# Splitting a V load of 128 partitions into one of 120 and one of 8, in an attention forward and backward kernel

## The chip, the cores and the metric

The kernel runs on one core of a Trainium2 chip. A core has TensorE (PE, whose weight loads are listed apart as PEld), VectorE (DVE), ScalarE (ACT), GpSimd (POOL) and SyncE (SP), which here issues every transfer, and 16 DMA engines that move the data between HBM and the on-chip memory SBUF. The metric is the device time of one execution in microseconds (us). Before the change it is 1648.51 us, the median of three runs (1648.39, 1648.51 and 1654.82).

## The reference

Two independent attention blocks, A and B, of the same shape, forward and backward. Per block there are 8 batches of 96 queries, 32 heads of width 128, and caches k and v of 512 keys. All in bfloat16. Cut to what matters:

```python
def _A_ref(x, k_cache, v_cache, wq, wo):            # _B_ref is the same
    B, Sq, D = x.shape                              # 8, 96, 640
    H, Dh = 32, 128                                 # Sk = 512
    q = (x @ wq).reshape(B, Sq, H, Dh).transpose(0, 2, 1, 3)
    scores = jnp.einsum("bhqd,bhkd->bhqk", q, k_cache) * (Dh ** -0.5)
    p = softmax(scores, axis=-1)
    o = jnp.einsum("bhqk,bhkd->bhqd", p, v_cache)
    return o.transpose(0, 2, 1, 3).reshape(B, Sq, H * Dh) @ wo

out = jnp.concatenate([A, B], axis=-1)
grads = vjp(out)(grad_out)      # dx, dk, dv, dwq, dwo of both blocks
```

The output and all ten gradients are returned. The caches are by far the largest inputs, and their gradients the largest outputs.

## The kernel before

**Tiling.** The unit of work is a chunk: one head of one batch of one block. A chunk has 96 queries on one side and 512 keys on the other. There are 2 x 32 x 8 = 512 chunks. Time is counted in ticks, one chunk a tick. Two neighbouring heads of a batch form a pair (HP = 2) and share their transfers, so that there are 256 pairs.

**Stages of a chunk.** c_s2a makes the scores S (L314) from Q and the transposed K and their maximum; c_s2b the exponential; c_s3a and c_s3b the probabilities P (L346, on GpSimd); c_s4 dV from P and dO (L387), which ScalarE copies to dV_sb (L392); c_s45 the output O from V and the transposed P (L362) and, in the same PSUM bank, the transpose of the next P (L369); c_s6 dP from the transposed V (L411) and dS (L415); c_s7 dK (L453), which ScalarE copies to dK_sb (L458); c_s78 dQ from K (L430) and the transpose of dS (L437). Between the chunks stand the steps of a head: projections (L250), natural copies, dwo (L491), dwq (L511), and groups of four heads that are multiplied with wo and wq into the output and dx (L536).

**Transfers.** Each pair needs V and K twice. Once they come transposed, KT_p and VT_p, by a transposing DMA (p_ldT, L277). Once they come as they are, V_sb and K_sb (p_ldn, L288): 128 partitions, each with four neighbouring keys of the two heads, so that a partition receives two runs of 1024 bytes, 256 KB in all. The gradients dV_sb and dK_sb go out in the same form (p_st, L297). A pair so has six transfers; in addition there are wq and wo slices (L199, L210), dwq and dwo (L518, L497), and inputs and outputs of x, the gradient and the result (L135, L141, L148, L552).

**Order.** Every step is put on a list with a tick and a slot, and the list is sorted. All transfers go through one chain on SyncE: the helper `sp` makes each one follow the one before it in issue order. For a pair whose first chunk has tick ct, the dictionary OFF has KT at ct-3, V at ct+1, VT at ct+2, K at ct+4, the store of dV at ct+7 and that of dK at ct+10. V is first read by c_s45 at ct+5, VT by c_s6 at ct+6, K by c_s78 at ct+9. Within SyncE's queue the six of different pairs interleave as KT, V, store of dV, VT, K, store of dK.

**Buffers.** V_sb, K_sb and VT_p have four buffers each, KT_p five, dV_sb four, dK_sb three. A load waits for the last reader of the buffer that it fills, a store for the copy that fills its tile. Completion is counted on eight semaphores in turn, so that each transfer also waits for the eighth before it.

The lines that the change touches are in p_ldn:

```python
    t_ = kvp.tile([128, HP, KC, 128], BF16, name=key, bufs=4)
    src = (kc if which == 0 else vc)[b, h:h + HP]
    sp(nc.sync.dma_start(t_[:].rearrange("p h c d -> p h (c d)"), src.rearrange("h (p c) d -> p h (c d)", c=KC)))
```

Of the kernel before, what the change touches and what calls it, by code (L numbers as in the profile page):

```python
# [77 lines left out]
def build_block(tc, em, tick0, blk, x, kc, vc, wq, wo, g_all, out_all, dx, dk, dv, dwq, dwo, ident, ones, pools, HG=4, first=True, groups=None):  # L78
    nc = tc.nc
# [7 lines left out]
    KC = Sk // 128  # L87
# [38 lines left out]
    sp = pools["sp"]  # L126
# [156 lines left out]
    def p_ldn(h, b, which):  # L283
        def f():
            key = "K_sb" if which == 0 else "V_sb"
            t_ = kvp.tile([128, HP, KC, 128], BF16, name=key, bufs=4)
            src = (kc if which == 0 else vc)[b, h:h + HP]
            sp(nc.sync.dma_start(t_[:].rearrange("p h c d -> p h (c d)"), src.rearrange("h (p c) d -> p h (c d)", c=KC)))  # L288
            for j in range(HP):
                CS[(blk, h + j, b)][key] = t_[:, j]  # L290
        return f
# [266 lines left out]
    for g in range(NG):  # L558
        h0 = GH0[g]
        for hh in range(groups[g]):  # L560
            h = h0 + hh
# [185 lines left out]
```

## Time and profile before

| What | us |
|---|---|
| Median of the runs | 1648.51 |
| The profiled execution, whole | 1642.09 |
| Its span, first to last instruction | 1640.3 |
| V_sb load, issue to landing (least, median, most) | 3.0, 4.3, 6.0 |
| K_sb load, the same | 3.0, 4.3, 6.7 |
| Transposing loads, the same | 3.1, 5.0, 7.4 |
| Stores of dV and dK, the same | 2.1, 4.4, 6.9 |
| Issue of a V_sb load on SyncE (least, median, most) | 0.38, 0.53, 1.68 |
| Issue of a transposing load (least, most) | 1.10, 3.94 |

The profile is of one execution, which was 6 us shorter than the median of the timed runs. Busy shares are parts of the span. A waits row tells which instruction waited, for whom, how long in total, how many times and the longest. SyncE does nothing but issue transfers, and its time is not counted as busy; the timeline of its queue shows each issue with its start and length. The DMA line gives, in 40 slices, the mean busy share of the 16 DMA engines; the queue rows give packets, megabytes and share. Queue q1 carries the program's own transfers, q8 and q14 carry instructions.

### The profile page before, as it was taken

To read this page: it belongs to the slowest core of one execution; us is meant where nothing else is said; L and a number is where in the kernel's file an instruction comes from. 1 tells how busy PE (TensorE), PEld (TensorE's weight loads), DVE (VectorE), ACT (ScalarE), POOL (GpSimd) and SP (SyncE) were. 2 spreads that over 40 slices of the span, in tenths; PEclk is the share of its full clock that TensorE was granted. 3 is DMA by queue.
4 is the path that set the end of the run, shared out by engine and by line. 5 is a ranking of instruction groups with operands and counts; after the bars stand their busy time and mean duration, and the time that the engine had idled before them with its cause. 6 is when DMAs were issued, how large, how long until landed. Compare 5 with 4: busy or idle time off the path is not lost.

```text
span 1640.3 us, 55387 instructions
## 1 busy us (share of the span) xinstructions
PE 1602.0 (98%) x20713; PEld 1262.0 (77%) x20906; DVE 1340.0 (82%) x3406; ACT 1346.9 (82%) x3498; POOL 532.3 (32%) x1026
## 2 busy tenths in 40 slices
PE   8899999999999999999999999999999999999998
PEld 6777877878777787777777778777787777877776
DVE  5876888888888888878778778888888888888796
ACT  7889988879788788877868889788788888889783
POOL 1333333333333333333323333333333333333331
PEclk9999999999999999999999999999999999999999
DMA  9999999999999999999999999999999999999995
GB/s 263 261 293 273 292 291 282 275 275 279 276 292 289 290 280 282 280 276 258 284 289 311 289 288 273 290 290 283 275 287 278 272 290 287 281 292 285 284 267 167
DMA packets 375566, 458.12 MB, mean 279 GB/s; under 512 B 40704, under 2 KB 367104, under 8 KB 367104
## 3 DMA queue, kind: packets, MB, share of 16 engines
q1 hardware_dynamic: 375296, 454.57, 103.2%
q8 instruction: 163, 2.67, 0.7%
q14 instruction: 107, 0.88, 0.1%
HBM read 160.10 MB, written 159.12 MB: 195 GB/s over the span
## 4 chain that ended last, share of the span: by engine, by line
PE 89%; DMA 4%; ACT 4%; issue 2%; DVE 1%; SPq 0%; POOL 0%; ACTq 0%; DVEq 0%
PE o_ps L536 12%; PE q_ps L250 12%; PE dwq_ps L511 6%; PE dK_ps L453 6%; PE dV_ps L387 6%; PE S_ps L314 6%; PE dwo_ps L491 6%; PE dP_ps L411 6%; PE optp_ps L362 5%; PE optp_ps L369 5%; PE dq_dst_ps L430 5%; PE dq_dst_ps L437 5%; PE n_ps L265 3%; PE nat_ps L477 2%; DMA out_dram<-dK_sb 2%
## 5 line engine op out<-in xcount | busy, mean ns | idle before, releaser
L401 POOL TENSOR_TENSOR prod<-OT_h,dOT_h 128x96 bf16<-128x96 bf16 x512 | 187.1, 365 | 824.4 <-DVE rinv L336 438.2
L346 POOL TENSOR_SCALAR P_sb<-E_sb,rinv 96x512 bf16<-96x512 bf16 x508 | 349.8, 689 | 252.5 <-DVE rinv L336 252.1
L458 ACT ACTIVATE dK_sb<-dK_ps 128x512 bf16<-128x512 f32 x512 | 305.4, 597 | 149.6 <-PE dK_ps L453 130.9
L326 ACT ACTIVATE E_sb<-S_ps,negm 96x512 bf16<-96x512 f32 x512 | 350.9, 685 | 65.1 <-DVE negm L316 51.8
L316 DVE TENSOR_REDUCE negm<-S_ps 96x1 f32<-96x512 f32 x512 | 347.6, 679 | 67.2 <-PE S_ps L314 66.5
L415 DVE SCALAR_TENSOR_TENSOR dS_sb<-dP_ps,dl_ps,P_sb 96x512 bf16<-96x512 f32 x512 | 380.6, 743 | 1.6 <-PE optp_ps L369 1.4
L392 ACT ACTIVATE dV_sb<-dV_ps 128x512 bf16<-128x512 f32 x512 | 307.2, 600 | 3.9 <-PE dV_ps L387 2.6
L376 ACT ACTIVATE PT_sb<-optp_ps 128x384 bf16<-128x384 bf16 x512 | 255.2, 499 | 1.7 <-PE optp_ps L369 0.8
L439 DVE COPY dST_sb<-dq_dst_ps 128x384 bf16<-128x384 bf16 x512 | 177.5, 347 | 53.1 <-PE dq_dst_ps L437 51.5
L387 PE MATMUL dV_ps<-dOnat_h,P_sb 96*128 96x128 bf16 x2048 | 199.7, 219 | 2.1 <-DVE ob L546 1.0
L453 PE MATMUL dK_ps<-Qnat_h,dS_sb 96*128 96x128 bf16 x2048 | 198.9, 219 | 0.1
L411 PE MATMUL dP_ps<-VT_p,dOT_h 128*96 128x512 bf16 x512 | 195.8, 382 | 0.0
L314 PE MATMUL S_ps<-KT_p,QT_h 128*96 128x512 bf16 x512 | 194.0, 379 | 0.5 <-ACT E_sb L326 0.2
L453 PEld LDWEIGHTS <-dS_sb 96*128 96x128 bf16 x2048 | 147.5, 97 | 48.3 <-issue 0.6
L430 PE MATMUL dq_dst_ps<-dST_sb,K_sb 128*128 128x96 bf16 x2048 | 171.8, 205 | 3.0 <-ACT dK_sb L458 2.8
L369 PE MATMUL optp_ps<-ident,P_sb 96*128 96x96 bf16 x2048 | 172.4, 206 | 2.2 <-DVE P_sb L346 1.6
L362 PE MATMUL optp_ps<-PT_sb,V_sb 128*128 128x96 bf16 x2048 | 169.6, 204 | 3.0 <-ACT PT_sb L376 0.9
L437 PE MATMUL dq_dst_ps<-ident,dS_sb 96*128 96x96 bf16 x2048 | 171.8, 205 | 0.0
L536 PE MATMUL o_ps<-wo_r,OT_h 128*128 128x128 bf16 (+1 forms) x722 | 144.5, 294 | 2.4
L536 PE MATMUL o_ps<-wqT_h,dQT_h 128*128 128x512 bf16 (+1 forms) x720 | 144.2, 294 | 2.5
L362 PEld LDWEIGHTS <-V_sb 128*128 128x128 bf16 x2048 | 107.6, 96 | 50.7 <-issue 3.4
L491 PE MATMUL dwo_ps<-g_nat,Onat 128*128 128x128 bf16 (+1 forms) x735 | 129.4, 297 | 4.3 <-ACT dK_sb L458 2.6
(75 smaller groups left out, 3044.7 us busy)
## 6 DMA issues: line engine op xcount, KB each, us to landing
out_dram<-dV_sb SPq DMA_DIRECT2D x256, 256.0 KB, 4.4
out_dram<-dK_sb SPq DMA_DIRECT2D x256, 256.0 KB, 4.5
V_sb<-in_A_v_cache_dram SPq DMA_DIRECT2D x128, 256.0 KB, 4.3
K_sb<-in_A_k_cache_dram SPq DMA_DIRECT2D x128, 256.0 KB, 4.4
V_sb<-in_B_v_cache_dram SPq DMA_DIRECT2D x128, 256.0 KB, 4.3
K_sb<-in_B_k_cache_dram SPq DMA_DIRECT2D x128, 256.0 KB, 4.3
out_dram<-ob SPq DMA_DIRECT2D x88, 160.0 KB, 4.1
out_dram<-dwq_sb SPq DMA_DIRECT2D x32, 320.0 KB, 4.9
```

The source lines that it names most:

```text
L314: nc.tensor.matmul(S_ps[:], hs["QT_h"][:, tok], st["KT"], start=True, stop=True)
L316: nc.vector.tensor_reduce(negm[:], S_ps[:], axis=AX.X, op=ALU.max, negate=True)
L326: nc.scalar.activation(E_sb[:].rearrange("q (a f) -> q a f", f=F4), st["S_ps"][:].rearrange("q (f a) -> q a f", f=F4), ACT.Exp, bias=st["n ...
L346: eng.tensor_scalar(P_sb[:], st["E_sb"][:], st["rinv"][:], 0.0, op0=ALU.mult, op1=ALU.add)
L362: nc.tensor.matmul(OT_ps, st["V_sb"][:, c, :], st["PT_sb"][:, c * Sq:(c + 1) * Sq], start=(c == 0), stop=(c == KC - 1))
L387: nc.tensor.matmul(dV_ps[:, c * 128:(c + 1) * 128], P_sb[:, c * 128:(c + 1) * 128], hs["dOnat_h"][:, b * 128:(b + 1) * 128], start=True, s ...
L392: nc.scalar.activation(dV_p[:, j], dV_ps[:], ACT.Identity, scale=1.0)
L411: nc.tensor.matmul(dP_ps[:], hs["dOT_h"][:, tok], st["VT"], start=True, stop=True)
L415: nc.vector.scalar_tensor_tensor(dS_sb[:].rearrange("q (a f) -> q a f", f=F4), dP_ps[:].rearrange("q (f a) -> q a f", f=F4), dl_ps[:, 0:1] ...
L453: nc.tensor.matmul(dK_ps[:, c * 128:(c + 1) * 128], dS_sb[:, c * 128:(c + 1) * 128], hs["Qnat_h"][:, b * 128:(b + 1) * 128], start=True, s ...
L458: nc.scalar.activation(dK_p[:, j], dK_ps[:], ACT.Identity, scale=1.0)
L536: nc.tensor.matmul(o_ps[:], src[:, t * 128:(t + 1) * 128], rhs, start=(hh == 0), stop=(hh == groups[g] - 1))
```

## The change

The load of V_sb is issued as two transfers, of partitions 0 to 119 and of 120 to 127. The load of K_sb stays one transfer. Nothing else changes: the tile, its buffers, the place in the chain and the bytes are the same. The first reader of V_sb now waits for two completions. SyncE's list grows from 1785 to 2041 rows, the 256 added issues; the orders on the other engines are the same.

```diff
             t_ = kvp.tile([128, HP, KC, 128], BF16, name=key, bufs=4)
             src = (kc if which == 0 else vc)[b, h:h + HP]
-            sp(nc.sync.dma_start(t_[:].rearrange("p h c d -> p h (c d)"), src.rearrange("h (p c) d -> p h (c d)", c=KC)))
+            dst = t_[:].rearrange("p h c d -> p h (c d)")
+            src = src.rearrange("h (p c) d -> p h (c d)", c=KC)
+            for (p0, p1) in (((0, 120), (120, 128)) if which == 1 else ((0, 128),)):
+                sp(nc.sync.dma_start(dst[p0:p1], src[p0:p1]))
             for j in range(HP):
                 CS[(blk, h + j, b)][key] = t_[:, j]
```

## The prediction

> **What bounds the kernel now.** I read the page first, then the waits of PE, then SyncE's queue, because the change touches that queue and the DMA engines alone. The page:
>
> ```profile
> span 1640.3 us, 55387 instructions
> PE 1602.0 (98%) x20713; PEld 1262.0 (77%) x20906; DVE 1340.0 (82%) x3406; ACT 1346.9 (82%) x3498; POOL 532.3 (32%) x1026
> DMA  9999999999999999999999999999999999999995
> ...
> q1 hardware_dynamic: 375296, 454.57, 103.2%
> q8 instruction: 163, 2.67, 0.7%
> ...
> PE 89%; DMA 4%; ACT 4%; issue 2%; DVE 1%; SPq 0%; POOL 0%; ACTq 0%; DVEq 0%
> ```
>
> Two resources are full at once: PE (98% busy, 89% of the chain) and the 16 DMA engines (every slice but the last at nine tenths or more; over 100% since packets overlap). Stages tell which of the two has something to spare:
>
> ```profile
> 200.00:600.00 400.00, 397.46 (x5201) 314.64 (x5248) 337.97 (x863) 335.30 (x874) 135.09 (x259) 1.00 1.06 283
> 770.00:920.00 150.00, 138.73 (x1779) 108.43 (x1797) 116.93 (x295) 118.24 (x308) 47.53 (x91) 0.99 1.05 292
> ```
>
> (Columns: stretch, length, busy PE, PEld, DVE, ACT, POOL, clock, DMA share, GB/s.) In the steady stretch PE idles 2.5 of 400 us; where block A hands over to block B it idles 11 of 150, and another 5 go between 60 and 110 us. The waits name the DMA stream as the cause there:
>
> ```profile
> ACT dK_sb L458 <- DMA out_dram<-dK_sb: 10.6, 6, 2.8
> PE dq_dst_ps L430 <- ACT dK_sb L458: 2.8, 1, 2.8
> PE optp_ps L362 <- DMA V_sb<-in_A_v_cache_dram: 0.8, 2, 0.4
> ```
>
> A store of dK lands late, its buffer isn't free, ScalarE waits and PE behind it. So all that a quicker DMA stream could win is about 5 + 9 = 14 us. What a slower one costs depends on its reserve. SyncE's queue, in a steady stretch:
>
> ```profile
> 1110.25 1.15 SPq L277 DMA_TRANSPOSE KT_p<-in_B_k_cache_dram  x1
> 1111.81 0.39 SPq L288 DMA_DIRECT2D V_sb<-in_B_v_cache_dram  x1
> 1112.30 0.40 SPq L297 DMA_DIRECT2D out_dram<-dV_sb  x1
> 1112.81 1.17 SPq L277 DMA_TRANSPOSE VT_p<-in_B_v_cache_dram  x1
> 1114.07 0.93 SPq L288 DMA_DIRECT2D K_sb<-in_B_k_cache_dram  x1
> 1115.09 0.42 SPq L297 DMA_DIRECT2D out_dram<-dK_sb  x1
> 1115.56 1.61 SPq L277 DMA_TRANSPOSE KT_p<-in_B_k_cache_dram  x1
> ```
>
> The issues stand end to end, with gaps of 0.05 to 0.1 us, from start to end of the run, and some are stretched (0.93 for a usual 0.53, 1.61 for 1.15). One pair of heads of one batch takes 6.22 us (the first V_sb issue is at 10.6 us, the last, number 256, at 1597.2). The queue's bare need for a pair: two transposes at 1.13, two loads at 0.53, two stores at 0.42, 0.46 for the 251 other issues shared out, and seven gaps of 0.1: 5.3 us. The other 0.9 us are stretched issues. They are not waits for buffers: I compared each issue with the last reader of the buffer that it fills, and for K and V loads that reader is done 1.3 to 15 us earlier. So the stream is never held by PE; it is held by the DMA engines, and it runs at its own pace, 6.22 us a pair, which happens to be PE's pace too. Its lead, from a V load's landing to the first L362 that reads it, is near 0 at 67 and 903 us and 4 to 10 us from 1000 us on. That is the whole reserve.
>
> [...]The page's 163 packets on q8 of 2.67 MB are 16 KiB each[...], one about every 10 us, and 0.7% of 16 x 1640.3 us over 163 gives 1.1 us each on whatever engine carries it.
>
> **The change, part by part.** Its aim would be to spare engine 15. The packet records of the trace show why one engine can matter: a transpose's packet takes 0.73 us on each engine when all come together, but about 2.0 us on fifteen of them when the sixteenth comes late, which is mostly after a q8 packet. Every transpose is thus a meeting of all engines, and the latest sets the pace. Which engine carries q8 no view tells.
>
> *Removed:* from engine 15, sixteen 1 KiB packets a pair at 46 ns (packet records), 0.74 us. A q8 block comes in about 160 of 512 intervals between transposes, half of them with a V load. If engine 15 is its carrier, 80 x 0.74 = 59 us leave the stream, 0.23 us a pair; if not, nothing does.
>
> [...]two packets more, 2 x 46 ns = 0.09 us a pair. That is the floor of the cost.
>
> *Changed way into SBUF:* unknown, and the trace has no such shape. [...]0.35.
>
> *SyncE:* 256 issues more. The cheapest load issue is 0.38, the usual 0.53, one gap more: 0.45 to 0.6 us a pair. The 0.9 us of stretching cover this; without that cover it would be 115 to 155 us. In 850 to 920 us, where the queue is densest, the issues' bare need leaves about 0.6 us a pair, still enough. Behind each added issue stand the dV store and the VT transpose.
>
> *Waits:* the first LDWEIGHTS on a V_sb now waits for two DMAs; one semaphore instruction more on PE, 51 ns in the trace and there beside running matmuls. I take 0; uncovered, 256 x 51 ns = 13 us. Each DMA also waits for the eighth before it: with seven a pair that lies 7.1 us back, against a V landing of 4.3 (median) and 6.0 (most): seldom felt, 0. Order on PE, DVE, ACT and POOL is unchanged.
>
> *Sum:* 256 x 0.35 = 90 us, less some 10 us of reserve: +80 us. From the profiled execution (1642.1 us in all, 1640.3 of it span) this gives 1722; the median before, 1648.5, is 6 higher, so 1728. I write 1725. PE should then idle for the difference, on V_sb and on stores.
>
> **Rivals.**
> 1. Relief: [...]The stream gains 0.23 - 0.09 x (share of intervals not set by q8) a pair, PE's 14 us of DMA-made idle mostly go: -8 to -12, 1638. For it: 59 us moved off nearly match what the late engine loses. Against: nothing names the engine. It decides only while the port cost stays under about 0.15 us a pair; above that it becomes slower than before. This is the case of the other sign.
> 2. Only the two packets: +0.09, some contention, to 0.15 us a pair: 23 to 38 less the reserve, +15 to +30, 1670.[...]
> 3. Full port sharing[...]. For it: the transposes line the engines up each time.
> 4. SyncE becomes the bound: if a transfer on fewer than 16 engines costs about twice as much to issue (1.1 us for each of the two), the queue needs 6.6 us a pair: 0.4 x 256 = +100, 1748. No row shows such a cost; it would show as V_sb issues over 0.6 us with little stretching elsewhere.
> That the transfers don't run on 15 and 8 engines would show in a packet count per transfer, and end near 2.
>
> **How the numbers follow.** The forecast (0.2 to 0.5 us a pair, +40 to +120) has 0.40, full sharing 0.18, two packets only 0.20, SyncE 0.10, relief 0.12. About what a measurement tells from no change is 0.5%, 8 us. Of relief, 0.10 is beyond that and 0.02 within; of the two packets 0.07 is within. So faster 0.10, same 0.09, slower 0.81. The range leaves out the relief and the upper part of full sharing: 1645 to 1815.
>
> **What would show it.** Right: V_sb's 1 KiB packets near 70 ns, fewer GB/s in the steady slices, PE under 97% there with idle ended by V_sb, VT_p or dK_sb, SyncE's transposes still stretched. Wrong towards relief: transposes' late arrivals after q8 fall, the leads grow, the idle of 770 to 920 us goes. Wrong towards SyncE: issues end to end with no stretched ones and DMA slices under nine. I would be wrong altogether if PE's steady idle stays at 2.5 in 400 us.

## The result, and the profile after

The changed kernel takes 1737.83 us (median of 4 runs, 1734.14 to 1743.05) against 1648.45 for the kernel before: 1.0536 times as long, 95% interval 1.0495 to 1.0576. By this ratio that is 88 us. The profiled execution took 1740.25 us, 1738.4 of it span.

The page of the changed kernel: span, the engines' busy time, the DMA slices, the queues and the chain that ended last.

```profile
span 1738.4 us, 55802 instructions
...
PE 1628.4 (94%) x20713; PEld 1276.6 (73%) x20906; DVE 1351.2 (78%) x3406; ACT 1353.3 (78%) x3498; POOL 532.8 (31%) x1026
...
DMA  9999999999999999999999999999999999999996
...
q1 hardware_dynamic: 377088, 454.58, 103.6%
q8 instruction: 164, 2.69, 0.7%
...
PE 73%; DMA 14%; ACT 6%; issue 3%; DVE 3%; SPq 1%; POOL 0%; ACTq 0%; DVEq 0%
```

The DMA engines look as full as before, every slice at nine tenths or more and 103.6%, although they move the same megabytes in 98 us more. So busy time alone hides the loss: the same bytes keep the engines busy for longer. PE's share of the chain fell from 89% to 73%, and DMA has 14% of it in place of 4%. Queue q1 has 1792 packets more than before, 7 for each of the 256 pairs. In the packet records these are the packets of 4 bytes, 36,864 before and 38,656 after. The 120 partitions alone (E3 below) leave 36,608 of them, one a pair fewer than before. The transfer of 8 leaves 8: in E5, where it has a queue of its own, that queue has 6144 packets, 24 a pair, 16 of them of 1 KiB. If a transfer leaves one on each engine that it uses, the two run on 15 and on 8 engines in place of 16. The transposes agree that one engine gets no V packet: in 241 of the change's 256 VT transposes the first of the 16 packets starts over 0.3 us ahead of the middle one, and the second does so in 2 (before, 3 and 3). Which engine it is the records don't tell; the number 15 was my assumption.

Stretches of the changed kernel (start and end, length, busy time of PE, PEld, DVE, ACT, POOL with counts, clock, DMA share, GB/s):

```profile
200.00:600.00 400.00, 381.99 (x4902) 299.73 (x4948) 321.54 (x814) 316.56 (x820) 126.25 (x242) 0.99 1.06 266
770.00:920.00 150.00, 133.89 (x1624) 103.41 (x1640) 106.72 (x267) 104.59 (x267) 40.21 (x78) 0.95 1.05 260
```

In the steady stretch PE idles 18.0 of 400 us, where it idled 2.5; the rate fell from 283 to 266 GB/s at the same DMA share of 1.06. The loss is spread over the whole run, not collected at the handover. Who waited (total us, times, longest):

```profile
ACT dK_sb L461 <- DMA out_dram<-dK_sb: 76.0, 42, 4.2
PE n_ps L265 <- ACT dK_sb L461: 20.5, 13, 2.5
PEld L365 <- DMA V_sb<-in_B_v_cache_dram: 17.0, 21, 2.2
PEld L365 <- DMA V_sb<-in_A_v_cache_dram: 15.4, 21, 1.7
PE dwo_ps L494 <- ACT dK_sb L461: 14.5, 15, 2.6
```

The row on dK_sb was 10.6 us in the kernel before: its store lands late, its buffer isn't free, ScalarE stands, and PE behind it. The rows on V_sb were 1.0 and 1.3 us. Both are symptoms of one stream that runs late; the rows don't tell whether SyncE issues it late or the engines move it slowly. SyncE's queue shows both:

```profile
1117.81 0.92 SPq L291 DMA_DIRECT2D V_sb<-in_B_v_cache_dram  x2
1118.82 0.41 SPq L300 DMA_DIRECT2D out_dram<-dV_sb  x1
1119.32 1.20 SPq L277 DMA_TRANSPOSE VT_p<-in_B_v_cache_dram  x1
1120.62 1.27 SPq L291 DMA_DIRECT2D K_sb<-in_B_k_cache_dram  x1
1121.98 0.41 SPq L300 DMA_DIRECT2D out_dram<-dK_sb  x1
1122.44 1.73 SPq L277 DMA_TRANSPOSE KT_p<-in_B_k_cache_dram  x1
```

The two V loads need 0.92 us where one needed 0.53 (median), and there are still stretched issues behind them (K 1.27, KT 1.73). Counted over 200 to 1500 us, a pair takes 6.70 us in place of 6.28. For the kernels below I took two things from the packet records: how long packets of 1 KiB (V, K and the two stores) last, and for how long in a pair fewer than 16 packets are in flight, that is, the 16 engines are not all supplied ("short").

```
kernel                      1 KiB packets   over 75 ns   mean ns   sum us   us/pair   short, us/pair
before                         262144          9380        51.9     13609     6.28        0.14
changed, 120 and 8             262144         44032        57.9     15191     6.70        0.29
E3   120 alone                 258048         40441        57.1     14722     6.40        0.07
E7   120, and 8 of 32 bytes    258048         40343        57.5     14846     6.57        0.33
E11  112 alone                 253952          9697        52.6     13346     6.28        0.26
E4   112 and 16                262144         10175        52.7     13828     6.50        0.38
E1   even and odd              262144         10772        52.3     13722     6.74        1.03
E2   halves                    262144         41848        57.5     15080     6.74        0.62
E6   one for each head         262144          9571        51.7     13560     6.40        0.40
E9   before, 8 DRAINs          262144         10477        52.3     13708     6.44        0.45
E10  before, 16 DRAINs         262144         11473        52.8     13853     6.77        1.01
E12  before, dV on ScalarE     262144          8780        50.9     13343     6.42        0.63
E8   changed, dV on ScalarE    262144         25560        53.6     14055     6.75        0.46
```

The change made 34,652 packets long; V has 65,536 of all. The long ones lie where V is: between a KT and the next VT transpose, where V and the store of dV run, 4,706 packets last over 75 ns before and 39,686 in the change, and elsewhere as many as before (4,674 and 4,346). The change also doubled the time in which the engines are short. The experiments take the two apart as far as they can.

### The profile page after: what moved, and what is told of

It reads as the page before. It is cut to its first block, busy times and chain, and to the rows that moved or that the text cites. A ratio compares the mean times of both kernels' runs of the same rounds, so it can differ in the third digit from the quotient of the medians.

```text
span 1738.4 us, 55802 instructions
## 1 busy us (share of the span) xinstructions
PE 1628.4 (94%) x20713; PEld 1276.6 (73%) x20906; DVE 1351.2 (78%) x3406; ACT 1353.3 (78%) x3498; POOL 532.8 (31%) x1026
## 3 DMA queue, kind: packets, MB, share of 16 engines
q1 hardware_dynamic: 377088, 454.58, 103.6%
## 4 chain that ended last, share of the span: by engine, by line
PE 73%; DMA 14%; ACT 6%; issue 3%; DVE 3%; SPq 1%; POOL 0%; ACTq 0%; DVEq 0%
PE o_ps L539 11%; DMA out_dram<-dK_sb 10%; PE q_ps L250 10%; PE dwq_ps L514 6%; PE dwo_ps L494 5%; PE S_ps L317 5%; PE dK_ps L456 5%; PE dV_ps L390 5%; PE dP_ps L414 4%; PE optp_ps L365 4%; PE optp_ps L372 4%; PE dq_dst_ps L433 4%; PE dq_dst_ps L440 4%; PE n_ps L265 3%; PE nat_ps L480 2%
## 5 line engine op out<-in xcount | busy, mean ns | idle before, releaser
L339 DVE RECIPROCAL rinv<-rowsum 96x1 f32<-96x1 f32 x512 | 78.1, 153 | 95.1 <-ACT E_sb L329 94.0
```

## The experiments

Two theories stood against each other. *Way into SBUF*: the loss is in the packets, because of how 120 and 8 partitions are dealt to engines. The expectations call it the ports theory, after an assumption of mine, that engines share ports on this way; no run shows it. *Issue time*: the loss is SyncE's, which has one transfer more to issue for each pair. Each experiment ran with the kernel before on the same chip (medians 1643.06, 1641.64 and 1642.20 us in the three sets), and ratios are to that.

**E1, E2: two transfers of 64 partitions, dealt in two ways.** Same number of transfers as in the change.

```diff
-for (p0, p1) in ((0, 120), (120, 128)):
-    sp(nc.sync.dma_start(dst[p0:p1], src[p0:p1]))
+for q in (0, 1):                                # E1
+    sp(nc.sync.dma_start(dst[q::2], src[q::2]))
+for (p0, p1) in ((0, 64), (64, 128)):           # E2
+    sp(nc.sync.dma_start(dst[p0:p1], src[p0:p1]))
```

> V in two transfers of 64 partitions, the even ones and the odd ones. Ports theory: [...]about as before, 1640 to 1665 us. Rival, the second issue or the second completion is the cost: as slow as the change, 1720 to 1750. Rival, fifteen engines or the uneven load of the engines is the cost: as before, 1645 to 1655.

> V in two transfers of 64 partitions, 0 to 63 and 64 to 127: the same number of transfers, packets per engine and issues as with even and odd partitions[...]. Ports theory: slow, [...]1710 to 1770. Rival, issue: equal to the even and odd split. Rival, fifteen engines or uneven load: as before, 1645 to 1655.

Measured: E1 1764.49 us, 1.0727 (1.0681 to 1.0774); E2 1762.87, 1.0742 (1.0688 to 1.0796). In packets they differ, 10,772 long ones against 41,848, and in time not at all. So the time of these two isn't set by packets. The queue of E1:

```profile
1112.43 1.29 SPq L291 DMA_DIRECT2D V_sb<-in_B_v_cache_dram  x2
1113.81 0.54 SPq L300 DMA_DIRECT2D out_dram<-dV_sb  x1
1114.45 1.12 SPq L277 DMA_TRANSPOSE VT_p<-in_B_v_cache_dram  x1
1115.67 1.15 SPq L291 DMA_DIRECT2D K_sb<-in_B_k_cache_dram  x1
1116.92 0.42 SPq L300 DMA_DIRECT2D out_dram<-dK_sb  x1
1117.39 1.24 SPq L277 DMA_TRANSPOSE KT_p<-in_B_k_cache_dram  x1
```

The two loads take 1.29 us here, 0.37 more than in the change, and the dV store behind them 0.54 in place of 0.41; the transposes are close to their bare 1.1 us, though the K load is still stretched (1.15). The engines were short for 1.03 us of each pair. Here SyncE's queue is nearly the bound, and in E2 the long packets cost nothing on top of it.

**E3, E4: the parts of the change.** E3 keeps the transfer of 120 alone, E4 splits at 112.

```diff
-for (p0, p1) in ((0, 120), (120, 128)):
+for (p0, p1) in ((0, 120),):                    # E3, and L365 reads [0:120]
+for (p0, p1) in ((0, 112), (112, 128)):         # E4
```

> V in one transfer of 120 partitions on 15 engines; partitions 120 to 127 are not loaded, and the product that makes the output O is taken over 120 of the 128 partitions, so keys are left out of O. Ports theory: [...]1680 to 1730. Rival, issue or two completions: as before, 1640 to 1650. Rival, the two packets more[...]: as before or a little quicker, 1630 to 1650, since the tail is gone.

> V in two transfers of 112 and of 16 partitions[...]. Ports theory: slow[...]: 1690 to 1750. Rival, fifteen engines or uneven load: as before, 1645 to 1655. Rival, issue: as the even and odd split.

Measured: E3 1670.44 us, 1.0173 (1.0156 to 1.0191); E4 1687.47, 1.0270 (1.0254 to 1.0286). E3 has one issue for each V load and a sixteenth less of V to move, its engines are short less than those of the kernel before (0.07), and it still loses 28 us: 40,441 of its packets are long. That loss is in the packets: from the end of a KT transpose to the start of the next VT transpose a pair takes 2.02 us in place of 1.68, and the packets in between took 0.34 us more for each engine and pair than as many did before (the transposes behind give back some 0.2 of it). E4 has as many transfers as the change and longer issues (0.53 and 0.45 us against 0.54 and 0.33), yet costs 44 us and not 88: its packets are short. None of its three expectations fits: the ports were expected to make it slow (1690 at least), the engines' load to leave it as before, and the issue to bring it to E1's 1764. Both theories hold in part.

**E5, E8: take work off SyncE's queue.** In E5 the transfer of 8 goes to ScalarE's queue, in E8 the dV stores do. E12 makes E8's move in the kernel before.

```diff
-sp(nc.sync.dma_start(dst[120:128], src[120:128]))
+nc.scalar.dma_start(dst[120:128], src[120:128])     # E5
...
-sp(nc.sync.dma_start(o_, t_[:]))
+nc.scalar.dma_start(o_, t_[:])                      # E8 and E12, for dV
```

> The changed kernel, but the transfer of the last 8 partitions is issued from ScalarE's queue; the 120 stay on SyncE. Packets, ports and engines are the same as in the changed kernel (1.054 times before), SyncE's queue is that of the kernel with the 120 partitions alone (1.017). Theory of issue time (the tail costs because SyncE has to issue it, 0.34 us and a gap of 0.1 a pair): 1.01 to 1.025, 1660 to 1685. Rival (the tail costs because its 16 packets of 1 KiB[...]): 1.045 to 1.06, 1717 to 1742. ScalarE's own queue gets 256 instructions more, so up to 0.01 on top of either.

> The changed kernel with the stores of dV issued from ScalarE's queue, so that SyncE has 0.5 us less to issue for each pair than in it and as many transfers as the kernel before. Issue time: most of the loss goes, 1.00 to 1.025, 1645 to 1685. Rival, the way of V into SBUF (packets at 102 ns in the 95th percentile, transposes waiting for a late engine): the loss stays, 1.04 to 1.06, 1710 to 1742.

> The kernel before with the stores of dV issued from ScalarE's queue: what that move costs or gives by itself, to read the same move made in the changed kernel (1.072, against 1.054 without it). SyncE has 0.5 us less to issue for each pair. If SyncE's time limits the kernel before: 0.99 to 1.00, 1628 to 1640, which would be better than both kernels. If waits on ScalarE's queue outweigh it, as they seem to there: 1.01 to 1.03, 1658 to 1690.

Measured: E5 1739.40 us, 1.0604 (1.0579 to 1.0629); E8 1759.21, 1.0722 (1.0691 to 1.0752); E12 1677.68, 1.0222 (1.0203 to 1.0241). Read alone, E5 and E8 would say that SyncE's time has no part in the loss. E12 weakens that reading: E8's move costs the kernel before 36 us by itself, with the shift of order that it brings. The waits of E5 show ScalarE having become late:

```profile
PE optp_ps L365 <- ACT PT_sb L379: 34.9, 20, 4.2
```

ScalarE stood over 0.1 us on the semaphore ahead of such an issue 18 times, 30 us in all and once for 4.98 us, and the issues themselves take it 0.28 us each. So in E5 a wait is taken away in one place and put into another, and E5 decides nothing about SyncE. The order of the instructions on ScalarE, VectorE and GpSimd also shifted: 735 of ScalarE's 3498 stand elsewhere in E5 than in the change.

E8 and E12 have the same order on these three engines (485 of ScalarE's moved), so they can be compared: with the dV stores on ScalarE the change costs 81 us, not much less than 88. SyncE has a transfer less to issue there, and the long packets are half as many: 16,780 more in E8 than in E12, nearly all of them on q1 (16,703) and not on the stores' own queue. So about half of the change's long packets are gone where the store of dV isn't in the same queue behind V. Neither theory explains why the loss stays. It speaks against SyncE's issue time as the whole of it, and ScalarE's lateness keeps it from deciding.

**E6: one transfer for each head.** The packets of the kernel before, with one issue more.

```diff
-sp(nc.sync.dma_start(dst, src))
+for j in range(HP):
+    sp(nc.sync.dma_start(dst[:, j], src[:, j]))
```

> The kernel before with each V load as two transfers of 128 partitions, one for each head: the same 256 packets of 1 KiB on the same 16 engines, one issue of about 0.53 us and a gap of 0.1 more a pair. Issue time: as the two transfers of 64 partitions, whose issues were of 0.6 us each, or somewhat less: 1.04 to 1.07, 1710 to 1760, and the transposes hardly stretched. Rival, ports and packets: nothing changes for them, 0.995 to 1.01, 1635 to 1660.

Measured: 1670.06 us, 1.0178 (1.0150 to 1.0207). It fits neither line. The V issues rise from 0.59 to 1.02 us a pair (mean), the sum of the 1 KiB packets is that of before (13,560 us), no order shifted, and 28 us are lost: an issue more costs something, but a quarter of its time only (0.49 x 256 = 125 us with its gap). ScalarE's wait for the stores of dK rises from 10.6 to 30.1 us. E1, with short packets and unshifted orders too, is the next point on this line: against E6 its V issues are 0.32 us a pair longer and the dV store 0.12, and it loses some 92 us more, 0.36 a pair, most of that length.

**E7: the tail without its bytes.** E3 with a second transfer of 32 bytes on each of the 8 partitions.

```diff
 sp(nc.sync.dma_start(dst[0:120], src[0:120]))
+sp(nc.sync.dma_start(dst[120:128, 0, 0:16], src[120:128, 0, 0:16]))
```

> V's 120 partitions as in the changed kernel, and the second transfer of 8 partitions kept but cut to 32 bytes on each of them: its issue stays, its 16 packets of 1 KiB become 8 of 32 bytes. O is summed over 120 of the 128 partitions, so the keys on the others are left out of it. With the 120 alone it was 1.017. Issue time: as the changed kernel, 1.04 to 1.055, 1710 to 1735. Rival, packets and ports of the tail: as the 120 alone, 1.015 to 1.025, 1668 to 1685.

Measured: 1710.50 us, 1.0415 (1.0396 to 1.0434). With E3 on one side and the change on the other, this lays the whole loss out in three steps, each of one edit and without a shift of order: the 120 partitions 28 us, the transfer of 8 as such 40, its bytes 20 (1.0536 - 1.0415 of 1642, 13 to 27 by the intervals). The bytes cannot explain the 40: 8 packets of 32 bytes and 8 of 4 a pair take 33 and about 22 us summed over all engines and the whole run. In its page DMA has the share of the chain that it has in the change:

```profile
PE 72%; DMA 15%; ACT 7%; issue 3%; DVE 2%; SPq 0%; POOL 0%; ACTq 0%; DVEq 0%
```

"DMA" on the chain so doesn't say slow engines: of E7's 68 us the larger part came with a transfer that moves next to nothing.

**E9, E10: time on SyncE's queue without a transfer.** Eight or sixteen DRAIN instructions, which move no data, after each V issue of the kernel before.

```diff
 sp(nc.sync.dma_start(dst, src))
+for _ in range(8 * which):                      # E10: 16
+    sp(nc.sync.drain())
```

> The kernel before with eight DRAIN instructions on SyncE after each V load's issue: time on SyncE's queue and no transfer, some 0.5 us a pair (two DRAINs at the end of the trace of before start 63 ns apart). If the 0.9 us of stretched issues are a reserve that covers such time, as the prediction has it: 0.995 to 1.01, 1635 to 1660. If they are no reserve: 0.5 x 256 = 128 us, 1.06 to 1.08. If it costs what the second issue of the per-head split cost (0.46 us and a gap, 28 us): 1.015 to 1.025.

> The same with sixteen DRAINs, some 1.0 us a pair. With a reserve of 0.9 us: 1.01 to 1.03. Without any: 1.13 to 1.16. If half of such time is covered by what stretching gives back, the loss is about twice that of the eight or more: 1.05 to 1.08, and the DMA engines run short of packets (fewer than 16 in flight) for about as long as is lost.

Measured: E9 1686.68 us, 1.0281 (1.0262 to 1.0300); E10 1761.79, 1.0744 (1.0722 to 1.0766). The queue of E9:

```profile
1115.73 0.53 SPq L288 DMA_DIRECT2D V_sb<-in_B_v_cache_dram  x1
1116.90 0.37 SPq L299 DMA_DIRECT2D out_dram<-dV_sb  x1
1117.36 1.93 SPq L277 DMA_TRANSPOSE VT_p<-in_B_v_cache_dram  x1
1119.38 0.53 SPq L288 DMA_DIRECT2D K_sb<-in_B_k_cache_dram  x1
```

From the end of the V issue (1116.26) to the store are 0.64 us, 0.1 of it usual: the eight took 0.54. From 200 to 1500 us the gaps in the queue rise from 0.62 to 1.18 us a pair, and to 1.63 with sixteen, while the issues themselves shrink from 5.69 to 5.25 and 5.15: stretching gave back 0.44 us of the first half microsecond and only 0.10 of the second. In time 0.56 us of the queue cost 46 us, 0.18 a pair, a third; 1.01 us cost 120, 0.47 a pair. The second half costs more than the first (0.29 of 0.45). And the 1.93 in the window shows that stretched issues don't all go away when SyncE has no time for them.

These two edits did more than fill SyncE's queue, though: 1336 of ScalarE's 3498 instructions stand elsewhere in E9 than before, 1438 in E10, and some of VectorE's and GpSimd's, where E1 to E4, E6, E7 and E11 shift none. The chain of E9:

```profile
PE 68%; ACT 16%; DVE 8%; DMA 5%; issue 3%; SPq 0%; POOL 0%; ACTq 0%; DVEq 0%; POOLq 0%
```

ScalarE and VectorE have 24% of it (5% before), and DMA has 5% (4% before, 14% in the change). How much of E9's 46 us is SyncE's time and how much the shifted order is therefore not shown. The step from E9 to E10 is nearer to SyncE's time alone: 277 of ScalarE's instructions differ in place, and PEld's waits for V_sb rise from 13 to 72 us.

The steady stretches of E9 and E10:

```profile
200.00:600.00 400.00, 394.27 (x5065) 306.36 (x5062) 330.13 (x835) 325.52 (x840) 130.93 (x249) 1.00 1.04 272
```

```profile
200.00:600.00 400.00, 383.07 (x4922) 296.82 (x4921) 322.49 (x811) 319.82 (x816) 126.82 (x242) 1.00 1.01 264
```

PE idles 5.7 and 16.9 of 400 us, without one transfer added and with packets hardly longer (51.9, 52.3 and 52.8 ns), and the DMA share falls (1.06, 1.04, 1.01). In these two the fall goes with a stream that is issued late. A share that stays doesn't rule that out: the change kept 1.06, and so did E7 (1.06), where most of the loss came with a transfer of next to no bytes.

**E11: 112 partitions alone.** The partner of E3, with 16 partitions left out in place of 8.

```diff
-for (p0, p1) in ((0, 120),):
+for (p0, p1) in ((0, 112),):                    # and L365 reads [0:112]
```

> V as one transfer of 112 partitions[...]; O is summed over 112 of the 128 partitions, so the keys on the others are left out of it. Compare with the 120 alone, on 15 engines, at 1.017. If the 120 lose by the way into SBUF that their deal gives (packets of 102 ns in the 95th percentile): these here have the packets of the 112 and 16 (65 ns there) and an eighth less of V to move, 0.98 to 1.00, 1610 to 1642. If any transfer of fewer than 128 partitions costs that much, or if the one engine without packets is the loss: 1.01 to 1.02 for the first, at most 1.00 for the second, whose packets would be short in the 120 too, which they were not.

Measured: 1637.22 us, 0.9964 (0.9951 to 0.9977). Stretches of E11 and of E3:

```profile
200.00:600.00 400.00, 399.87 (x5248) 314.54 (x5247) 338.06 (x864) 335.44 (x873) 135.13 (x258) 1.00 1.05 278
```

```profile
200.00:600.00 400.00, 392.07 (x5100) 309.18 (x5145) 331.94 (x847) 328.36 (x853) 131.74 (x252) 1.00 1.07 276
```

With an eighth less of V, PE idles 0.1 of 400 us; with a sixteenth less but on 15 engines it idles 7.9, at a higher DMA share. (The trace of E3 lacks 45 matmul records of this stretch, as those of before and of the change lack some, so 2 or 3 us of such idle may be records.) So the loss of E3 isn't the price of every transfer under 128 partitions, but of this deal. Whether it is the fifteen engines or the partitions that each writes is not tried apart in time; long packets at least need no transfer of 120 partitions, E2's two of 64 have 41,848. E11 also prices what relief of the DMA engines could bring at all: 5 us.

No experiment gave a version that beats both kernels; E11 leaves keys out, and E12, the one try to free SyncE in the kernel before, lost 36 us.

## Why the prediction was right, and where it was not

*The sum* came out: 1725 was written, 1737.83 measured, inside the range, +80 against +88. That it came so near is luck: the way into SBUF was put at 90 us and measured at 48, SyncE's issue was put at 0 and the second transfer measured at 40, and the two errors nearly cancel.

*What bounds the kernel now.* DMA engines and PE full at once, with some 10 us of reserve and at most 14 to win. E11 won 5, which fits; the reserve was tried by no run.

*Removed: 0.74 us a pair from one engine, worth 59 us if that engine carries q8, else nothing.* Nothing. In the changed kernel an engine with no V packets reaches the transpose early, so the starts of a transpose's 16 packets show it: the first lies 252 us (summed over the run) ahead of the middle one, against 18 before, while the last lies 276 us behind it, against 281. The freed engine only waits. In 74 of the 80 stretches up to a VT transpose that hold a q8 packet one engine came over 0.5 us early and another over 0.5 us late: the carrier of q8 isn't the engine that was freed. Rival 1, the relief, falls with this.

*Added by two packets more on each of eight engines: 0.09 us a pair, 23 us.* E7 against the change: 20.

*Changed way into SBUF: taken 0.35 us a pair for both transfers.* This was my estimate; what it rested on was not shown. In time this is E3's 28 us and the 20 of the tail's bytes, 48 us or 0.19 a pair: the forecast was nearly twice too large. The deal alone may be a little dearer than 28, since E3 moves less. Slower packets are there, but the reason given for them, shared ports, is not shown, and no run tells another. By split, packets above 75 ns are over 40,000 with the 120 partitions (40,441) and the halves (41,848), and about 10,000 with the 112 (9,697), the 112 and 16 (10,175) and the even and odd partitions (10,772). The packets of the tail of 8 are short: E5 has them on a queue of their own, and 224 of 4096 last over 75 ns. And in E8, where the store isn't behind V in the queue, half of the long packets are gone. The sum of 1 KiB packets grew by 1582 us; if all of that were V's, its 65,536 packets would be 24 ns longer, 76 ns by the mean of before, where 70 was foretold.

*SyncE: 0.45 to 0.6 us a pair, covered by 0.9 us of stretched issues, cost 0.* This is the step that failed. The price of the issue was about right: 0.33 us (median) and a gap. The cover wasn't: stretched issues gave back a part, and less the more was added (0.44 us a pair for E9's 0.56, 0.10 for the next 0.45 of E10). E6's added issue cost 28 us, a quarter of its length, and E1's further 0.44 us most of theirs, both with packets and orders as before; E9 and E10 point the same way, with a shifted order beside. For the transfer of 8, E7 puts the price at 40 us, 0.16 a pair, for some 0.4 us of queue. By E6's quarter such time would cost some 25 us in the kernel before. The rest may come with the 120's slower packets or with something else that a second transfer brings; that was not tried apart, and E8 against E12 says that a lighter queue alone doesn't bring it back.

*Waits: 0.* No run separates the second completion on PE from V that lands late; the 32 us of PEld on V_sb contain both. E6 has the second completion and the seventh transfer a pair too, so what they cost there is within its 28 us.

*Rivals.* Two packets only (1670) fell short by the deal and by the second transfer. Full port sharing was an estimate of mine above the forecast, and so further still from the 48 us. Rival 4 looked in the right place but had a wrong sign to know it by: no V issue of the change is above 0.6 us in the median and stretched issues stay, and still the second transfer as such cost 40 us. Its sum is off as well: two issues of 1.1 us and a gap more in place of one of 0.53 make 5.3 us a pair into 7.1, not 6.6. With issues of 0.6 us and hardly stretched transposes, it is what E1 and E2 are.

*What would show it.* PE under 97% in the steady slices (95.5), idle ended by V_sb and dK_sb, stretched transposes: all there. They were signs of "the stream is late", and fit both causes. What tells more are the packets' lengths and the time in which engines are short.

## What to carry to other kernels

Where two units fed each other in turn, here SyncE's queue and the DMA engines, time in which one was held up by the other was no reserve: price added work on either at a part of its length (here a quarter for an added issue of half a microsecond, most of the next 0.44) instead of at nothing. Splitting the transfer paid for its issue (28 us in E6, with packets as before), and which partitions a transfer took went with the length of its packets: 112 alone had 9,697 over 75 ns and took 1637 us against 1642 for the kernel before, 120 alone had 40,441 and took 28 us more than it. So look at the packets' lengths before choosing a split. A probe that adds instructions to one queue can move those on others, as E9 did with 1336 of ScalarE's 3498: compare the orders before a loss is put down to the queue. To relieve one engine of sixteen, first show that it is the late one; here an engine that came 252 us early to the transposes, summed over the run, gave that time away.

## What the runs showed of the hardware

- The issue of a V load on SyncE differed with its shape, and not in the order of size (medians): 128 partitions 0.53 us, 120 0.54, 64 0.60 to 0.62, 16 0.45, 8 0.33, one head of 128 partitions 0.43 as the second of two. After two transfers of 64 the dV store takes 0.55 us in place of 0.42.
- On ScalarE's queue the 8 partitions took 0.28 us to issue (median) and dV stores 0.38, and none was stretched beyond 0.59, while SyncE's V loads reach 1.7 before and 2.0 in E5; but ScalarE waited up to 4.98 us ahead of one.
- A packet of 1 KiB took 46 ns in the median in every kernel, and 102 ns at the 95th percentile in the change, 59 before: the split shows in the slowest packets only.
- At a transpose after a q8 packet the last engine came 1.2 to 1.4 us behind the middle one, in the mean, 160 to 162 times a run and 198 to 225 us in all, whatever was done to V.
